# First attention of an attention and feed-forward kernel: maximum and sums through TensorE products

## The chip, the core and the metric

The kernel runs on one core of one Trainium2 chip. The metric is the device time of one execution, in microseconds (us). A profiled execution also has a span, from its first to its last instruction in the trace; all starts in the rows below count from the span's start.

## What is computed

For every batch b (8), and every head (8 heads, 64 wide, 576 tokens), the reference makes 32 "memories" and attends over them; then all tokens go through a feed-forward layer.

```python
a = phi - max(phi over tokens); a = exp(a); a = a / (sum over tokens + 1e-9)
k_m = a.T @ k;  v_m = a.T @ v                    # 32 x 64 per head
scores = (q @ k_m.T) / 8                         # 576 x 32 per head
scores = scores - max(scores over the 32)
attn = exp(scores); attn = attn / (sum over the 32 + 1e-9)
x = heads side by side of (attn @ v_m)           # 4608 x 512
out = max(x @ w_in, 0) ** 2 @ w_out              # w_in 512 x 2048, w_out 2048 x 512
```

## The kernel before, in words

Tokens are worked in 16 half-batches (b, t) of T = 288. The partitions of an attention tile hold 4 heads x 32 memories: "half" 0 and 1 are the even and odd heads of the four pairs, so one half-batch's attention is a tile of 128 x (2 x 288). `attn @ v_m @ w_in` is regrouped: `u = v_m @ w_in` is made per batch (`make_u`, L514), and `ffn1` (L642) multiplies it by the attention; `ffn2` (L669) multiplies the squared result by w_out. Weights arrive packed and are decoded on chip (`decode`, L545): ScalarE writes two intermediate tiles (L556, L559), VectorE reworks one (L563, L565, L568), and VectorE or GpSimd adds them (L575).

The time around the change is the start, before the first `ffn1`. It is written out by hand as generators, advanced in the order of one string (L1265): `e` is the softmax over tokens of batch 0, `m` its memories, `d0`, `d1`, `d2` three decodings of w_in, `o0` one of w_out, `a0` and `a1` the attention of half-batches (0, 0) and (0, 1), `u0` and `v0` two parts of u for batch 0, and `s` a spin.

```python
"e e e e e m m d0 m m d0 a0 a0 d1 a0 s d1 d0 a0 d1 s d2 a0 u0 d2 a0 u0 d2 s a1 o0 o0 v0 v0 s"
```

Each engine issues its instructions in the order in which this string brings them to it, and waits in order. A spin (`spin`, L148) is a product of the identity with itself that nothing reads. An fp32 product is two TensorE instructions (load and product each), so `spin(1)` is two instructions of 512 columns, and the eight products of `by_heads` (L418) are sixteen.

The first attention before, `attend` (L430), in six steps for `a0`: scores by `by_heads` into two PSUM banks (TensorE); two block transposes out of PSUM (L443) and the maximum over blocks of 32 (L448), then four spins; the subtraction (L453, VectorE here); the exponential (L455, ScalarE); the sum, eps, reciprocal (L458 to L460), two spins, the multiplication (L463); and the transposition back (L468). The result is the fp32 tile `a_hi2`, which `ffn1` reads. While the start lasts, `new_ps` (L131) hands out PSUM banks `acc0`/`acc1` and `acc2`/`acc3` in turns.

The start ends in three products that the first feed-forward steps need: the attention tile (L468), the second part of u (`v0`, L424 and L525, behind the addition of `d2`, L575), and the first decoded w_out (`o0`, whose addition L575 comes right after the string).

Of the kernel before, what the change touches and what calls it, by code (L numbers as in the profile page):

```python
# [9 lines left out]
F32 = mybir.dt.float32  # L10
# [3 lines left out]
AF = mybir.ActivationFunctionType  # L14
ALU = mybir.AluOpType
AX = mybir.AxisListType
# [9 lines left out]
def attn_moe_kernel(ctx: ExitStack, tc: tile.TileContext, qT, kv, phi, w_in, w_out, outT):  # L26
# [12 lines left out]
    nc = tc.nc  # L39
    ctx.enter_context(tc.manual_schedule())  # L40

    B, NQ, S = kv.shape[:3]
    P = 128
    DM = outT.shape[0]
    NPAIR = 2 * NQ
    DFF = w_out.shape[0]
    D = 64
    M = 32
    NFT = DFF // P
    NET = DM // P  # L50
    T = S // 2
# [9 lines left out]
    EPS = 1e-9  # L61
    SCALE = 1.0 / float(D) ** 0.5
# [4 lines left out]
    const = ctx.enter_context(tc.tile_pool(name="const", bufs=1))  # L67
    work = ctx.enter_context(tc.tile_pool(name="work", bufs=2))
    one = ctx.enter_context(tc.tile_pool(name="one", bufs=1))
    dram = ctx.enter_context(tc.tile_pool(name="dram", bufs=1, space=bass.MemoryType.DRAM))  # L70
    ps_acc = ctx.enter_context(tc.tile_pool(name="ps_acc", bufs=1, space=PSUM))
    ps_h = ctx.enter_context(tc.tile_pool(name="ps_h", bufs=2, space=PSUM))
# [3 lines left out]
    ident = const.tile([P, P], F32, name="ident")  # L76
# [45 lines left out]

    eps = const.tile([P, NQ * NBLK], F32, name="eps")
    nc.gpsimd.memset(eps, EPS)

    kv_used = set()
    starting = [True]
# [3 lines left out]
    def new_ps(main=False):  # L131

        if starting and not main:
            n = len(starting) - 1
            starting.append(True)
            return [ps_acc.tile([P, 512], F32, name=f"acc{2 * (n % 2) + i}") for i in range(2)]
        assert not ps_user, (now, ps_user)
        ps_user.append(list(now))
        return ps_m.tile([P, 2, 512], F32, name="ps_m")

    def done_ps(ps):
        if not isinstance(ps, list):
            ps_user.pop()

    def bank(ps, i):
        return ps[i] if isinstance(ps, list) else ps[:, i]

    def spin(n, x):  # L148

        h = ps_h.tile([P, 512], F32, name="h")  # L150
        for _ in range(n):
            nc.tensor.matmul(h, x, ident[:, None, :].broadcast_to([P, 4, P]), start=True, stop=True)
# [38 lines left out]
    def exp_phi(b, e):  # L191

        w = NQ * P
        mx = chunk_max(e)
        yield
        ps = new_ps()
        tp, bc = bank(ps, 0), bank(ps, 1)
        for qd in range(NQ):
            nc.tensor.transpose(tp[:, qd * P:(qd + 1) * P], mx[:, qd * P:(qd + 1) * P], ident)
        yield  # L200
        nmx = work.tile([P, NQ], F32, name="nmx")
        nc.vector.tensor_reduce(
            out=nmx, in_=tp[:, :w].rearrange("p (q x) -> p q x", q=NQ), axis=AX.X, op=ALU.max, negate=True
        )
        yield
        for qd in range(NQ):
            nc.tensor.matmul(
                bc[:, qd * P:(qd + 1) * P], nmx[:, qd:qd + 1].broadcast_to([P, P]), ident,
                start=True, stop=True,
            )  # L210
        if starting:
            spin(1, nmx[:, :1].broadcast_to([P, P]))
        yield
        if starting:
            for x in e:
                n = x.shape[0]
                nc.vector.tensor_tensor(out=x, in0=x, in1=bc[:n, :w], op=ALU.add)
                nc.scalar.activation(x, x, AF.Exp)
        else:
            n = e[4].shape[0]  # L220
            nc.vector.tensor_tensor(
                out=e_sb[:, :4], in0=e_sb[:, :4], in1=bc[:, None, :w].broadcast_to([P, 4, w]), op=ALU.add
            )
            nc.vector.tensor_tensor(out=e[4], in0=e[4], in1=bc[:n, :w], op=ALU.add)
        done_ps(ps)
        if starting:
            ready.add(("phi", b))
            return
        yield
        nfull = S // P  # L230
        nc.scalar.activation(e_sb[:, :nfull], e_sb[:, :nfull], AF.Exp)
        if nfull < NCH:
            nc.scalar.activation(e[nfull], e[nfull], AF.Exp)
        ready.add(("phi", b))
# [60 lines left out]
    def memories(b, e, kvs, mem):  # L295
# [6 lines left out]
        sums = [(ps_h.tile([P, 512], F32, name="h") if qd else tp) if not b else accs[qd][:, 2 * D:] for qd in range(NQ)]  # L302
# [39 lines left out]
        if two:  # L342
            n = rows(NCH - 1)
            for j in range(4):
                for qd in range(NQ):
                    y = kvs[qd][-1] if qd else kvs[qd][-1][:n]
# [22 lines left out]
        for qd in turns:  # L369
            x = accs[qd][:, :2 * D].rearrange("p (x d) -> p x d", x=2)[:, :, None, :].broadcast_to([P, 2, 2, D])  # L370
# [9 lines left out]
        if b > 2:  # L380
            done_ps(ps)
            for j in range(4):
                if j == 2 or j and b > JOIN:
                    yield
                for k in range(2):
                    for x in range(2):
                        at = M * (2 * (j % 2) + k)
# [12 lines left out]
        for half, copy in ((0, nc.scalar.copy if b == 1 else nc.vector.tensor_copy), (1, nc.scalar.copy)):  # L400
            hs = slice(D * half, D * (half + 1))
            copy(mem[hs], tp[hs].rearrange("p (x r h m) -> p x r h m", x=2, r=NPAIR, h=2)[:, :, :, half])
        done_ps(ps)
        ready.add(("mem", b))

    def load_q(b, t):
        if (b, t) in ((0, 1), (1, 1)):
            x = [const.tile([P, NQ, T], F32, name=n) for n in ("a_hi3", "a_lo3")]
        else:
            x = one.tile([P, NPAIR, T], F32, name="q_sb")  # L410
            x = [x[:, :NQ], x[:, NQ:]]
        for i in range(2):
            nc.sync.dma_start(
                out=x[i], in_=qT[b, NQ * i:NQ * (i + 1), :, t * T:(t + 1) * T].rearrange("a p s -> p a s")
            )
        return x

    def by_heads(out, mem, x, rhs):  # L418

        for pr in range(NPAIR):  # L420
            for half in range(2):
                hs = slice(D * half, D * (half + 1))
                y = rhs[pr // NQ][hs, pr % NQ]
                nc.tensor.matmul(  # L424
                    bank(out, half)[M * pr:M * (pr + 1), :y.shape[-1]], mem[hs, x, pr], y, start=True, stop=True
                )
# [65 lines left out]
    def new_a():  # L492
        i = a_slots.take()
        return (const.tile([P, NQ, T], F32R, name=f"a_hi{i}"), const.tile([P, NQ, T], F32R, name=f"a_lo{i}"), i)
# [8 lines left out]
    ready = set()  # L503
# [92 lines left out]
    def decode_in(n, q0, q1, adder=nc.gpsimd):  # L596

        def new_out():
            if n // 2 not in w_in_at:
                w_in_at[n // 2] = new_w()  # L600
            return w_in_at[n // 2][:, 2 * q0:2 * q1, n % 2 * HC:n % 2 * HC + HC]

        assert all(("in", n, qd) in fetched for qd in range(q0, q1))
        yield from decode(raws["in", n][:, q0:q1], new_out, adder, ("in", n, q0))
        ready.update(("in", n, qd) for qd in range(q0, q1))
        if all(("in", n ^ i, x) in ready for i in range(2) for x in range(NQ)):
            if starting:
                kept.append(n // 2)
                return
            yield  # L610
            keep_w(n // 2)

    def decode_out(k, adder=nc.gpsimd, whole=False):

        def new_out():
            w = room(k, [P, 2, DM], F32)
            wo[2 * k:2 * k + 2] = [w[:, 0], w[:, 1]]
            return w

        assert all(("out", k, i) in fetched for i in range(2))  # L620
        w = yield from decode(raws.pop(("out", k)), new_out if whole else None, adder, ("out", k))
        if not whole:
            yield
            yield from split(k, w.rearrange("p (i x) -> p i x", i=2))
        ready.update(("out", 2 * k + i) for i in range(2))
# [475 lines left out]
    state = {b: {"a32": {}, "q": {}, "u": {}, "a": [None] * NT, "kv": {}} for b in range(B)}  # L1101
# [16 lines left out]
    def task_mem(b, kvs=None):  # L1118
        kvs = kvs or [state[b]["kv"][qd] for qd in range(NQ)]
        new_mem(b)  # L1120
        return memories(b, [e_sb[:, c] for c in range(NCH)], kvs, state[b]["mem"])
# [6 lines left out]
    def task_attend(b, t):  # L1128
        def new():
            state[b]["a"][t] = new_a()  # L1130
            return state[b]["a"][t]

        return attend(b, t, state[b]["q"].pop(t), state[b]["mem"], new)
# [14 lines left out]
    def task_u(b, n, n0=0, n1=FC):  # L1148
        got = state[b]["u"].setdefault(n, [])
        w = w_at.pop((b, n)) if (b, n) in w_at else w_in_at[n]  # L1150
        if (b, n) not in streamed:
            assert all(("in", 2 * n + i, qd) in ready for i in range(n0 // HC, n1 // HC) for qd in range(NQ))
        return make_u(b, n, state[b]["mem"], (n0, n1, w), got)

    full = {0}
    unsplit = {(0, 0): "a_hi2", (0, 1): "u_lo0"}
# [28 lines left out]
    st = state[0]  # L1185
# [59 lines left out]
    for fn, *args in loads[:later]:  # L1245
# [5 lines left out]
    start = {  # L1251
        "e": lambda: exp_phi(0, st["phi"]),
        "m": lambda: task_mem(0, kvs),
        "d0": lambda: decode_in(0, 0, 1),
        "d1": lambda: decode_in(0, 1, 2),
        "d2": lambda: decode_in(1, 0, 2, nc.vector),
        "o0": lambda: decode_out(0, nc.vector, True),
        "v0": lambda: task_u(0, 0, HC, 2 * HC),
        "a0": lambda: task_attend(0, 0),
        "a1": lambda: task_attend(0, 1),  # L1260
        "u0": lambda: task_u(0, 0, 0, HC),
    }
# [175 lines left out]
    for k, step in enumerate(steps):  # L1438
        i, b, t, f = step
# [57 lines left out]
    for j in range(-1, LAST + 1):  # L1497
# [29 lines left out]
        if new:  # L1527
            ffn1_product(u1, j + 1, 1, True)
            ffn1_product(z, j + 1, 2, True)
            x = from_z(j + 1, 2, *(("g_hi", 3) if old else ("r", 2)))  # L1530
# [99 lines left out]
```

## Time and profile before

| | |
|---|---|
| time, median of 3 runs | 703.32 us (702.68 to 704.96) |
| time of the profiled execution | 703.33 us |
| its span | 701.5 us |
| TensorE products busy | 688.9 us (98%) |
| TensorE weight loads busy | 568.9 us (81%) |
| VectorE busy | 517.6 us (74%) |
| ScalarE busy | 407.2 us (58%) |
| GpSimd busy | 353.3 us (50%) |

TensorE's weight loads run beside its products. A busy TensorE is not one at its peak, since products are pipelined and the time of one (272 ns) is longer than the distance to the next. An engine's share over the whole span says little of one stage; the rows below are mostly of the first 50 us. "Idle before" in brackets names what the trace takes for the releaser of a wait.

### The profile page before, as it was taken

To read this page: it belongs to the slowest core of one execution; us is meant where nothing else is said; L and a number is where in the kernel's file an instruction comes from. 1 tells how busy PE (TensorE), PEld (TensorE's weight loads), DVE (VectorE), ACT (ScalarE), POOL (GpSimd) and SP (SyncE) were. 2 spreads that over 40 slices of the span, in tenths; PEclk is the share of its full clock that TensorE was granted. 3 is DMA by queue.
4 is the path that set the end of the run, shared out by engine and by line. 5 is a ranking of instruction groups with operands and counts; after the bars stand their busy time and mean duration, and the time that the engine had idled before them with its cause. 6 is when DMAs were issued, how large, how long until landed. Compare 5 with 4: busy or idle time off the path is not lost.

```text
span 701.5 us, 13957 instructions
## 1 busy us (share of the span) xinstructions
PE 688.9 (98%) x5030; PEld 568.9 (81%) x5030; DVE 517.6 (74%) x1138; ACT 407.2 (58%) x1117; POOL 353.3 (50%) x527
## 2 busy tenths in 40 slices
PE   7889999999999999999999999999999999999997
PEld 3367889899998887888788878877888778888897
DVE  3977759644775979988798979887998876765432
ACT  2566888876455455655565456655565556554531
POOL 1122345443376557745774568555764577555100
PEclk9999999999999999999999999999999999999999
DMA  9996154704346561069114911375105300400101
GB/s 300 356 348 242 58 191 129 249 1 139 119 100 208 149 179 60 16 198 231 44 56 154 257 71 61 112 215 155 62 26 189 91 28 37 146 36 0 47 15 45
DMA packets 65365, 89.83 MB, mean 128 GB/s; under 512 B 6928, under 2 KB 53584, under 8 KB 61712
## 3 DMA queue, kind: packets, MB, share of 16 engines
q1 hardware_dynamic: 63408, 87.41, 39.6%
q10 hardware_dynamic: 1888, 1.54, 0.7%
q8 instruction: 39, 0.64, 0.4%
q14 instruction: 30, 0.25, 0.1%
HBM read 75.30 MB, written 13.63 MB: 127 GB/s over the span
## 4 chain that ended last, share of the span: by engine, by line
PE 92%; DMA 4%; DVE 2%; ACT 0%; issue 0%; SPq 0%; DVEq 0%; ACTq 0%
PE acc L1004 39%; PE h L1028 11%; PE acc L682 10%; PE z L1028 8%; PE h L653 7%; PE acc L674 4%; PE m L424 4%; PE h L1580 2%; DMA wp<-in_w_in 1%; PE ps_m L424 1%; DMA wp<-in_w_out 1%; PE m L1580 1%; PE z L1580 1%; DMA kvb<-in_kv 1%; PE m L316 1%; PE acc L1469 1%
## 5 line engine op out<-in xcount | busy, mean ns | idle before, releaser
L1004 PE MATMUL acc<-u_hi,wp 128*128 128x512 f32 x576 | 154.4, 399 | 0.0
L1004 PE MATMUL acc<-u_lo,wp 128*128 128x512 f32 x576 | 147.7, 392 | 0.0
L1004 PEld LDWEIGHTS acc<-u_hi,wp 128*128 128x128 f32 x576 | 103.8, 188 | 41.4 <-issue 24.1
L1004 PEld LDWEIGHTS acc<-u_lo,wp 128*128 128x128 f32 x576 | 105.6, 188 | 18.4
L909 POOL TENSOR_TENSOR u_lo<-low,u_hi 128x256 fp32r<-128x256 f32 (+1 forms) x134 | 84.8, 644 | 51.7 <-ACT u_hi L908 50.4
L1052 POOL TENSOR_TENSOR u_hi<-g_lo,u_hi 128x288 fp32r<-128x288 f32 (+1 forms) x82 | 64.7, 789 | 73.5 <-ACT g_lo L1049 50.8
L666 POOL TENSOR_TENSOR g_lo<-g,g_hi 128x288 fp32r<-128x288 f32 x48 | 44.5, 929 | 65.6 <-ACT g_hi L664 51.4
L908 ACT CAST u_hi<-low 128x256 fp32r<-128x256 f32 (+1 forms) x160 | 51.9, 347 | 43.7 <-POOL low L920 21.0
L682 PE MATMUL acc<-g_hi,wp 128*128 128x288 f32 x360 | 58.7, 297 | 0.9 <-DVE o L1085 0.9
L1047 ACT ACTIVATE u_hi<-g_hi 128x224 fp32r<-128x224 f32 x95 | 39.0, 410 | 35.0 <-DVE g_hi L1044 35.0
L682 PEld LDWEIGHTS acc<-g_hi,wp 128*128 128x128 f32 x360 | 51.1, 188 | 5.3 <-issue 2.6
L1044 DVE CUSTOM_DVE_ANT_0 g_hi<-h,g_hi 128x288 f32<-128x288 f32 x95 | 42.7, 450 | 4.9 <-ACT g_hi L1075 4.2
L655 ACT ACTIVATE r<-h 128x288 f32<-128x288 f32 x64 | 26.1, 407 | 33.7 <-PE h L653 33.4
L1052 POOL TENSOR_TENSOR u_lo<-g_lo,u_lo 128x224 fp32r<-128x224 f32 x30 | 21.5, 715 | 38.3 <-ACT g_lo L1049 36.5
L1075 ACT COPY g_hi<-z 128x288 f32<-128x288 f32 x48 | 19.1, 397 | 28.7 <-PE z L1028 28.6
L1028 PE MATMUL z<-a_hi,u_hi 128*128 128x288 f32 x120 | 35.3, 294 | 0.0
L1028 PE MATMUL h<-a_lo,u_hi 128*128 128x288 f32 x120 | 34.6, 295 | 0.0
L682 PE MATMUL acc<-g_lo,wp 128*128 128x288 f32 x180 | 34.6, 295 | 0.0
L674 PE MATMUL acc<-g_hi,wp 128*128 128x288 f32 x128 | 34.0, 410 | 0.6 <-DVE wp L575 0.6
L1067 ACT ACTIVATE u_lo<-g 128x288 fp32r<-128x288 f32 x48 | 21.4, 446 | 22.3 <-DVE g L1063 22.1
L1028 PE MATMUL h<-w_sb,u_hi 128*128 128x288 f32 x120 | 34.1, 296 | 0.0
L1069 DVE TENSOR_TENSOR g_lo<-h,g 128x288 f32<-128x288 f32 x48 | 21.8, 454 | 14.9 <-ACT g L1065 13.3
(340 smaller groups left out, 1785.4 us busy)
## 6 DMA issues: line engine op xcount, KB each, us to landing
w_sb<-w_f SPq DMA_DIRECT2D x24, 1024.0 KB, 5.0
wp<-in_w_in SPq DMA_DIRECT2D x16, 512.0 KB, 7.8
wp<-in_w_out SPq DMA_DIRECT2D x16, 512.0 KB, 7.1
q_sb<-in_q SPq DMA_DIRECT2D x28, 288.0 KB, 5.6
kvb<-in_kv SPq DMA_DIRECT2D x28, 256.0 KB, 6.3
tmp<-in_kv SPq DMA_DIRECT2D x24, 256.0 KB, 5.9
w_f<-w_sb SPq DMA_DIRECT2D x4, 1024.0 KB, 5.0
e_sb<-in_phi SPq DMA_DIRECT2D x7, 512.0 KB, 6.5
```

The costliest lines, as they stand in the source:

```text
L424: nc.tensor.matmul(bank(out, half)[M * pr:M * (pr + 1), :y.shape[-1]], mem[hs, x, pr], y, start=True, stop=True)
L653: nc.tensor.matmul(h[:, :T], u[:, qd, fs], x[:, qd], start=(i == 0), stop=(i == len(todo) - 1))
L666: nc.gpsimd.tensor_tensor(out=g_lo, in0=g, in1=g_hi.bitcast(F32), op=ALU.subtract)
L674: nc.tensor.matmul(acc[e][:, :T], wo[f][:, e * P:(e + 1) * P], g_hi, start=first, stop=last)
L682: nc.tensor.matmul(acc[e][:, :T], wo[f][:, w, e * P:(e + 1) * P], x, start=first and x is g_hi and w == 0, stop=last and x is g_lo,)
L908: nc.scalar.copy(hi[:, k], x)
L909: by(name, p).tensor_tensor(out=lo[:, k], in0=x, in1=hi[:, k].bitcast(F32), op=ALU.subtract)
L1004: nc.tensor.matmul(late_accs[e], wo[f][:, w, e * P:(e + 1) * P], x, start=f == 0 and first, stop=f == NFT - 1 and last,)
L1028: nc.tensor.matmul(out[:, :T], u[:, lhs], a, start=first and not n, stop=n == 2, skip_group_check=not first)
L1044: nc.vector._custom_dve(TENSOR_ADD_SAT, out=x, in0=u[:, :T], in1=x, s0=float("inf"), s1=0.0)
L1047: nc.scalar.square(g_hi, x[:, :n])
L1052: by(f"c{k}", p).tensor_tensor(out=g_lo, in0=g[:, :n], in1=g_hi.bitcast(F32), op=ALU.subtract)
```

## The change

`a0` calls a new generator `first_attend` in place of `attend`; nothing else moves in the order string. It has five steps where `attend` had six, and the sixth `a0` of the string does nothing.

1. TensorE: 24 products with 96 tokens as stationary columns (64 partitions) and 32 memories as moving columns, so that scores stand with tokens on partitions (`by_token`); then the old scores (`by_heads`) into the other two banks; then a spin.
2. VectorE: two maxima over blocks of 32 straight from PSUM, 96 x 384 each, negated. TensorE: `spread`, 24 products (32 stationary columns, 96 moving) that add the negated maximum onto the old scores in PSUM; then a spin.
3. ScalarE: two exponentials from PSUM, 128 x 288 each. TensorE: 6 products with 96 stationary columns and 4 moving ones (`heads`, a 0/1 matrix) that give the sums with tokens on partitions.
4. VectorE: add eps, reciprocal, on 96 x 24. TensorE: `spread` again, 24 products, into two banks.
5. VectorE: two multiplications, PSUM by SBUF, 128 x 288 each, into `a_hi2`.

Five memsets on GpSimd at the start make `heads`.

```diff
+    heads = const.tile([P, P // M], F32, name="heads")
+    nc.gpsimd.memset(heads, 0.0)
+    for g in range(P // M):
+        nc.gpsimd.memset(heads[M * g:M * (g + 1), g:g + 1], 1.0)
...
+    def first_attend(q, mem):
...
+        C = 3
+        R = T // C
+        G = P // M
+        by_token = new_ps()
+        for c in range(C):
+            for pr in range(NPAIR):
+                for half in range(2):
+                    hs = slice(D * half, D * (half + 1))
+                    at = M * (G * c + pr)
+                    nc.tensor.matmul(
+                        bank(by_token, half)[:R, at:at + M], q[pr // NQ][hs, pr % NQ, R * c:R * (c + 1)], mem[hs, 0, pr],
+                        start=True, stop=True,
+                    )
+        sc = new_ps()
+        by_heads(sc, mem, 0, q)
+        spin(1, ident)
+        yield
+        mx = const.tile([P, 2, C, G], F32, name="tops")
+        for half in range(2):
+            y = bank(by_token, half)[:R, :C * P].rearrange("t (c g m) -> t c g m", c=C, g=G)
+            nc.vector.tensor_reduce(out=mx[:R, half], in_=y, axis=AX.X, op=ALU.max, negate=True)
+
+        def spread(out, x, **kw):
+            for half in range(2):
+                for c in range(C):
+                    for g in range(G):
+                        nc.tensor.matmul(
+                            bank(out, half)[M * g:M * (g + 1), R * c:R * (c + 1)],
+                            x[:R, half, c, g:g + 1].broadcast_to([R, M]), ident[:R, :R], stop=True, **kw
+                        )
+
+        spread(sc, mx, start=False, skip_group_check=True)
+        spin(1, ident)
+        yield
+        y = one.tile([P, 2, T], F32, name="st")
+        for half in range(2):
+            nc.scalar.activation(y[:, half], bank(sc, half)[:, :T], AF.Exp, scale=SCALE)
+        sums = ps_h.tile([P, 512], F32, name="h")[:R, :2 * C * G].rearrange("t (h c g) -> t h c g", h=2, c=C)
+        for half in range(2):
+            for c in range(C):
+                nc.tensor.matmul(sums[:, half, c], y[:, half, R * c:R * (c + 1)], heads, start=True, stop=True)
+        yield
+        nc.vector.tensor_scalar_add(mx[:R], sums, EPS)
+        nc.vector.reciprocal(mx[:R], mx[:R])
+        out = new_ps()
+        spread(out, mx, start=True)
+        yield
+        at = const.tile([P, NQ, T], F32, name=unsplit[0, 0])
+        state[0]["a32"][0] = at
+        for half in range(2):
+            nc.vector.tensor_tensor(out=at[:, half], in0=bank(out, half)[:, :T], in1=y[:, half], op=ALU.mult)
+        ready.add(("a32", 0, 0))
...
-        "a0": lambda: task_attend(0, 0),
+        "a0": lambda: first_attend(state[0]["q"].pop(0), state[0]["mem"]),
```

## Rows read from the trace of the kernel before

**Rows 1.** The page's part 2, forty equal slices of the span

```profile
PE   7889999999999999999999999999999999999997
...
DVE  3977759644775979988798979887998876765432
```

**Rows 2.** Stretches: length, busy us of PE, PEld, DVE, ACT, POOL; PEclk

```profile
18.50:22.00 3.50, 3.37 (x9) 1.25 (x8) 3.36 (x8) 1.76 (x3) 1.27 (x1) 1.00 1.04 402
...
41.00:46.50 5.50, 3.79 (x126) 2.96 (x124) 5.35 (x7) 2.95 (x6) 0.00 (x0) 1.00 1.04 378
46.50:60.00 13.50, 13.50 (x88) 9.00 (x96) 8.97 (x15) 8.87 (x19) 4.90 (x3) 1.00 0.93 350
```

**Rows 3.** The chain that ended last: start us, us, what

```profile
32.03 1.23 DVE wp L575
...
41.04 1.22 DVE e_sb L221
...
46.49 2.21 PE acc L674 x8
```

**Rows 4.** Timeline (start us, us), VectorE: first attention and a decoding

```profile
18.43 0.84 DVE L443 STREAM_TRANSPOSE st<-acc 128x288 f32<-128x288 f32 x2
...
23.86 0.27 DVE L460 RECIPROCAL sm<-sm 128x18 f32<-128x18 f32 x1
...
24.16 0.76 DVE L463 TENSOR_TENSOR st<-st,sm 128x576 f32<-128x576 f32 x1
...
24.83 0.69 DVE L563 TENSOR_SCALAR tmp<-tmp 128x1024 f32<-128x1024 f32 x1
...
27.43 0.77 DVE L468 STREAM_TRANSPOSE a_hi<-st 128x576 f32<-128x576 f32 x1
...
28.12 1.18 DVE L575 CUSTOM_DVE_ANT_0 w_sb<-tmp,low 128x2048 uint16<-128x2048 uint16 x1
```

**Rows 5.** Timeline, TensorE's weight loads: scores, and a spin between scores

```profile
17.44 0.18 PEld L424 LDWEIGHTS acc<-q_sb,mem 64*32 64x32 f32 x14 [0.27 <-ACT mem L402]
...
18.09 0.30 PEld L152 LDWEIGHTS h<-ident 128*128 128x128 f32 x2 [0.46 <-issue]
...
26.75 0.30 PEld L152 LDWEIGHTS h<-ident 128*128 128x128 f32 x2 [0.41 <-issue]
...
27.80 0.12 PEld L424 LDWEIGHTS acc<-a_hi,mem 64*32 64x32 f32 x4 [0.76 <-DMA e_sb<-in_phi]
```

**Rows 6.** Timeline, TensorE: products with 32 stationary columns

```profile
13.72 0.28 PE L307 MATMUL h<-ones,e_sb 128*32 128x2 f32 x16
...
13.85 0.41 PE L316 MATMUL acc<-u_lo,e_sb 128*32 128x128 f32 x8
...
14.29 0.28 PE L307 MATMUL h<-ones,e_sb 128*32 128x2 f32 x16
```

**Rows 7.** Timeline, TensorE: four loads of 128 columns

```profile
7.22 0.52 PEld L207 LDWEIGHTS acc<-ident,nmx 128*128 128x128 f32 x4 [0.75 <-DVE nmx L202]
```

**Rows 8.** One tile's instructions, ns min/median/max: narrow loads and products

```profile
L316 PEld LDWEIGHTS acc<-wp,e_sb x40: 106/110/110, 10.3 to 14.7; 128*32 128x32 f32 x40
L316 PE MATMUL acc<-wp,e_sb x40: 272/273/297, 10.3 to 14.8; 128*32 128x128 f32 x40
```

**Rows 9.** Timeline and page: prices of single instructions

```profile
6.74 0.42 DVE L202 TENSOR_REDUCE nmx<-acc 128x2 f32<-128x256 f32 x1 [0.58 <-PE acc L199]
...
32.18 0.41 ACT L655 ACTIVATE r<-h 128x288 f32<-128x288 f32 x1 [1.13 <-PE h L653]
...
L1069 DVE TENSOR_TENSOR g_lo<-h,g 128x288 f32<-128x288 f32 x48 | 21.8, 454 | 14.9 <-ACT g L1065 13.3
```

**Rows 10.** Timeline: GpSimd at the start, ScalarE at the second decoding

```profile
1.28 0.12 POOL L124 MEMSET eps<- 128x18 f32 x1
...
18.69 1.27 POOL L575 TENSOR_TENSOR w_sb<-tmp,low 128x512 int32<-128x512 int32 x1 [15.15 <-DVE tmp L568]
...
22.41 1.15 ACT L556 ACTIVATE tmp<-wp 128x1024 f32<-128x1024 f32 x1 [0.85 <-DMA wp<-in_w_in]
```

More of the change, by code (lines that the diff above doesn't have):

```diff
@@ L404, in memories @@
         ready.add(("mem", b))
+    def first_attend(q, mem):
+        assert ("mem", 0) in ready
+        C = 3
[48 more added lines that the diff above has]
+        ready.add(("a32", 0, 0))
```

## The prediction, made before the changed kernel ran

> **What bounds the kernel now.** I read the forty slices first [rows 1]: TensorE is at 9 from the fourth slice to the last but one, so only the first 50 us have room, and there VectorE is the busy one (a 9 in the second slice). The stretches of the start say it sharper [rows 2]: from 41.0 to 46.5 us VectorE works 5.35 of 5.5 us and TensorE 3.79; from 46.5 us TensorE is busy without a gap. The chain that ended last [rows 3] then shows VectorE's addition for w_out at 32.03, its work for batch 1 at 41.04, and TensorE from 46.49 on. So whatever moves VectorE's line before 33 us moves the end by the same amount: behind it stand VectorE's own queue and then a full TensorE. (Earlier pieces of the chain name DMA transfers. I don't take these as waits: VectorE's instructions follow one another there without idle time.)
>
> The place to watch is the second large decoding, `d2`. Its first VectorE instruction begins at 24.83, right behind the first attention's multiplication at 24.16; its addition begins at 28.12, behind the transposition L468 [rows 4]. `v0` and `o0` follow that addition in order. I measure the change by when that addition can begin.
>
> **What is removed.** Nine VectorE instructions of `a0` (L443 twice, the last L468, 0.77 us) [rows 4], 5.6 us of VectorE together, and four of the six spins inside `a0`. In the old kernel no step of `a0` made VectorE wait: its transposes began at 18.43, when VectorE came free of `d0`.
>
> **What is added.** VectorE gets two maxima, an addition, a reciprocal and two multiplications. The maxima: 256 columns from PSUM took 0.42 us; for 384 I take 0.55 each (bounds 0.42, and 0.63 by straight scaling). The multiplications have a twin in L1069, 288 columns with one PSUM operand, 0.45 us each [rows 9]. The reciprocal cost 0.27 [rows 4]; the addition has no more columns, 0.2. In sum 2.5 us, so VectorE's work falls by 3.1 us. But each new step sits behind TensorE, VectorE keeps its order, and everything behind a waiting instruction waits too: `d1` behind the maxima, `d2` behind the multiplications. So the new line is TensorE's, and I add it up.
>
> *Start.* The products need the second half of `mem`, copied by ScalarE; the scores' loads went on at 17.44 [rows 5]. The same holds now.
>
> *By token.* 48 instructions, each with a load of 96 columns on 64 partitions. No row has this shape. Four loads of 128 columns span 0.52 us with 0.19 for the last, 111 ns apart [rows 7], or 0.87 ns a column: 83 ns for 96 columns. The moving side, 32 columns, is shorter than that. Loads into separate tiles of the array do overlap: sixteen products of 32 stationary columns passed in 0.13 us, 8 ns apart, though one load lasts 110 ns [rows 6, 8]; and 14 loads on two halves of the rows spanned 0.18 us [rows 5]. Even and odd heads lie on the two halves and alternate, so I take two at a time: 48 x 83 / 2 = 2.0 us, ending at 19.5. Bounds: 48 x 8 ns = 0.4 us, and 48 x 111 ns = 5.3 us. I take the value between because the load is nearest in width to [rows 7] and in placing to [rows 5]. [...]
>
> *Scores, spin.* The old scores again: 0.65 us from 17.44 to the next load at 18.09. A spin: 26.75 to 27.80, 1.05 us [rows 5]. That is 21.2 us. Beside it run the maxima: a product's result comes 0.16 us after its streaming (273 ns [rows 8] against four times 27 ns [rows 6]), so 19.7 + 1.1 = 20.8: hidden by the spin. `d1`, behind them on VectorE, takes about half of `d2`'s 2.5 us (24.83 to 28.12 without L468) and is done near 22.1, GpSimd's addition for it 1.3 us later [rows 4, 10]: early enough for all that follows.
>
> *First spread.* 48 instructions of 96 columns over four column tiles. Sixteen with 128 columns plus their change-over fill 13.85 to 14.29, 27 ns each [rows 6]; scaled to 96 columns 21 ns: 1.0 us, and 0.1 to change over; ends at 22.3. (Bounds 8 and 29 ns.) *Spin*: 23.35. The exponentials, 0.41 us each [rows 9], start half by half and end at 22.9: hidden by this spin. ScalarE then goes to `d2`, whose data landed only at 22.41 [rows 10]; a start at 22.9 ends its first pass at 24.1, before VectorE asks.
>
> *Sums.* 12 instructions with 96-column loads on all rows, nothing to overlap with: 12 x 83 ns = 1.0 us, 24.35 (bounds 0.1 and 1.3). The addition and reciprocal follow until about 25.0, hidden by the `s` spin, which ends at 25.4. *Second spread*: 1.1 us, 26.5; result and hand-over 0.2; the last multiplication 0.45 (the first runs beside the spread's second half): 27.2.
>
> So `d2` begins on VectorE at 27.2 where it began at 24.83: 2.35 us later. Between it and its addition L468 is gone, 0.77 us: the addition is **1.6 us later**. ScalarE's second pass for it has ended by then (its buffer comes free when GpSimd ends `d1`, near 23.4). On TensorE, `u0`'s products stand behind the second spread and one spin; they too are later, but `v0` behind them waits for the addition of `d2` in any case. Nothing behind gives this back: VectorE's queue from `o0` to 46.5 us is the same work in the same order [rows 2, 3].
>
> *At nothing:* the five memsets, 0.1 us each like the one at 1.28, on a GpSimd that later idles for 15.15 us before 18.69 [rows 10]; uncovered they would cost 0.6 us. No DMA is added or moved on any queue, and the first scores of `a1`, which take the next pair of banks, come after the exponentials.
>
> **Sum.** 703.3 + 1.6 = **704.9 us**, against the profiled execution's 703.33 (span 701.5 and 1.8 around it), which is also the median of the runs. About 0.3%, 2.1 us, is what a measurement of this kernel can tell from no change: I forecast a loss below that. By the pitches' spread, half a microsecond in by-token and about as much in the rest, this case's own range is 703.9 to 705.9.
>
> **Rivals.** *Slower: the wide loads don't overlap.* The place is the by-token products. If a 96-column load holds the array's load path alone, 48 x 83 ns = 4.0 us, 2.0 more; the maxima no longer hide, and all behind moves: 3.6 us later, 706.9 us. It decides from 52 ns an instruction (by token 2.5 us, a loss of 2.1). For it: the path for wide loads isn't shown shared in any row. Against: narrow loads overlap in both directions. [...]
>
> *Faster or equal: the products are as cheap as the narrow ones.* By token 0.4 us and sums 0.4 us; then VectorE's maxima set the pace (18.43 + 1.1 = 19.5), and by the same sum `d2` begins at 25.0 and its addition 0.6 us earlier: 702.7 us. At the far end VectorE's saving would count until ScalarE's first pass of `d2`, 22.41 + 1.15 = 23.56 [rows 10]: 1.3 + 0.77 = 2.0 us, 701.3. For it: the 8 ns of narrow products [rows 6]. Against: a load four times as long is not in those rows.
>
> *The clock falls.* [...] The new stretch has fewer spins, small products and waits. [...] Against: by my sum TensorE waits nowhere for long.
>
> **Chances.** Forecast 0.57, serial loads 0.21, cheap products 0.17 (0.05 of it near its far end), clock 0.05. Slower by over 0.3% (above 705.4): the serial case, the clock, and a sixth of the forecast: 0.36. Faster by over 0.3% (below 701.2): only the far end, 0.05. Within: 0.59. The range that leaves out 2 in 10 goes from the cheap case to just beyond the serial one: 702.4 to 707.2.
>
> **What would show it.** Right: by-token products some 42 ns apart, ending near 19.5; VectorE idle for about a microsecond before the maxima, and again, some 2 us in all, before the sums' addition and the multiplications, with TensorE as the releaser; L563 of `d2` near 27.2 and its addition near 29.7; the first `ffn2` 1.6 us after its old place, and the same distance at 46.5 us. Wrong: by-token spacing of 8 or of 80 ns; maxima that end after the spin; a granted clock below 1.00 between 17 and 30 us; or a shift at 30 us that is no longer there at 60 us, which would mean that VectorE's line was not what the end hung on.

## The result, and the profile after

The changed kernel took 710.86 us (median of 4 runs, 710.36 to 710.96); the kernel before took 703.87 (median of the three runs of the table above and one more). The ratio is 1.0098 with an interval of 1.0079 to 1.0117: 5.6 to 8.2 us slower. I had said 704.9 and at most 707.2. In a run in which TensorE's granted clock fell the time is longer (one kernel below took 704.12 to 704.46 us at 1.000, and in the median 707.96 at 0.995 to 0.998); since that is one of the causes here, runs are told apart by the clock that each lists.

The page of the changed kernel, part 2, against [rows 1]: the same picture, but the second slice has a PEclk of 8, and VectorE has fallen from 9 to 5 there.

```profile
PE   7989999999999999999999999999999999999997
...
DVE  3597659744866878988798879887997877755432
...
PEclk9899999999999999999999999999999999999999
```

The stretches behind it (length, then busy us and number of instructions of PE, PEld, DVE, ACT, POOL, then the granted clock, DMA share and GB/s), to set beside [rows 2]:

```profile
17.00:18.50 1.50, 1.50 (x32) 1.50 (x32) 0.73 (x2) 0.15 (x1) 0.56 (x1) 0.81 1.09 384
18.50:22.00 3.50, 3.50 (x34) 1.76 (x32) 2.24 (x5) 1.18 (x2) 0.71 (x1) 0.50 1.04 403
22.00:26.00 4.00, 4.00 (x55) 2.48 (x54) 0.23 (x1) 1.45 (x3) 1.78 (x2) 0.65 1.03 391
26.00:31.00 5.00, 5.00 (x80) 2.78 (x80) 2.75 (x7) 1.67 (x3) 0.00 (x0) 1.00 1.08 341
```

The reader is to see three things in them. The granted clock is 0.50 for all of 18.5 to 22.0, and partly before and after (0.81 and 0.65). TensorE is busy for every microsecond of it (3.50 of 3.50), so no wait of TensorE shows. VectorE works 0.23 of the 4 us from 22 to 26: it waits, and it is TensorE that it waits for (4.70 us before the addition, L456 below). A cut at 17.95 and at 24.78 gives a clock of 0.50 throughout those 6.83 us.

The timeline of the same stretch (start us, us, engine, line; L423 by-token loads, L434 maxima, L157 spins, L440 spread, L454 sums, L456 addition, L464 multiplications, L624 the first VectorE instruction of `d2`, L636 its addition, L735 the first product of the second layer):

```profile
16.69 2.84 PEld L423 LDWEIGHTS acc<-mem,q_sb 64*96 64x96 f32 x46 [0.16 <-ACT mem L407]
...
19.69 1.02 DVE L434 TENSOR_REDUCE tops<-acc 96x12 f32<-96x384 f32 x2 [1.93 <-PE acc L423]
...
20.74 2.07 PE L157 MATMUL h<-ident 128*128 128x512 f32 x2
...
22.74 2.15 PE L440 MATMUL acc<-ident,tops 96*32 96x96 f32 x48
...
24.82 1.13 PE L157 MATMUL h<-ident 128*128 128x512 f32 x2
...
25.79 1.10 PE L454 MATMUL h<-heads,st 128*96 128x4 f32 x12
...
26.93 0.18 DVE L456 TENSOR_SCALAR tops<-h 96x24 f32<-96x24 f32 x1 [4.70 <-PE h L454]
...
27.78 1.20 PE L440 MATMUL acc<-ident,tops 96*32 96x96 f32 x48
28.62 0.95 DVE L464 TENSOR_TENSOR a_hi<-acc,st 128x288 f32<-128x288 f32 x2 [1.18 <-PE acc L440]
...
29.49 0.68 DVE L624 TENSOR_SCALAR tmp<-tmp 128x1024 f32<-128x1024 f32 x1
...
32.33 1.23 DVE L636 CUSTOM_DVE_ANT_0 w_sb<-tmp,low 128x2048 uint16<-128x2048 uint16 x1 [0.17 <-PE acc L485]
...
37.66 2.18 PE L735 MATMUL acc<-g_hi,wp 128*128 128x288 f32 x8 [0.29 <-DVE wp L636]
```

The first spin lasts 2.07 us and the first spread 2.15; the second ones, after 24.8, 1.13 and 1.20. `d2` begins at 29.49, where it began at 24.83 [rows 4]; the first second-layer product comes at 37.66, where it came at 33.41: 4.25 us later. The line of that product in the kernel before:

```profile
33.41 2.18 PE L674 MATMUL acc<-g_hi,wp 128*128 128x288 f32 x8 [0.29 <-DVE wp L575]
```

That distance lies unchanged in the chain where VectorE's line ends and TensorE's begins, 50.75 against 46.49 [rows 3]:

```profile
49.47 1.24 DVE wp L636
...
50.75 2.21 PE acc L735 x8
```

But the span is 708.5 us against 701.5: 7.0 us. Another 2.75 us are lost later, and not in a wait. They are in the 1152 products of 512 columns, which took 399 and 392 ns each before (the two groups, `u_hi` and `u_lo`) and now take 401 and 394, 1.3 us of busy time more in each group. Before, then after:

```profile
L1004 PE MATMUL acc<-u_hi,wp 128*128 128x512 f32 x576 | 154.4, 399 | 0.0
L1004 PE MATMUL acc<-u_lo,wp 128*128 128x512 f32 x576 | 147.7, 392 | 0.0
```

```profile
L1065 PE MATMUL acc<-u_hi,wp 128*128 128x512 f32 x576 | 155.7, 401 | 0.0
L1065 PE MATMUL acc<-u_lo,wp 128*128 128x512 f32 x576 | 149.0, 394 | 0.0
```

So there were three losses to explain, and only one of them was in my sum.

### The profile page after: what moved, and what is told of

It is laid out like the page before. It is cut to its first block, busy times and chain, and to the rows that moved or that the text cites. A ratio compares the mean times of both kernels' runs of the same rounds, so it can differ in the third digit from the quotient of the medians.

```text
span 708.5 us, 14256 instructions
## 1 busy us (share of the span) xinstructions
PE 695.9 (98%) x5178; PEld 575.5 (81%) x5178; DVE 514.1 (73%) x1135; ACT 407.1 (57%) x1118; POOL 353.8 (50%) x532
## 4 chain that ended last, share of the span: by engine, by line
PE 95%; DVE 3%; DMA 1%; ACT 0%; issue 0%; SPq 0%; DVEq 0%; ACTq 0%
PE acc L1065 39%; PE h L1089 11%; PE acc L743 10%; PE z L1089 8%; PE h L714 7%; PE acc L735 4%; PE m L485 4%; PE h L1641 2%; PE ps_m L485 1%; PE z L1641 1%; PE m L1641 1%; PE h L157 1%; PE m L321 1%; PE acc L1530 1%; PE h L321 1%; PE h L485 1%
## 5 line engine op out<-in xcount | busy, mean ns | idle before, releaser
L735 PE MATMUL acc<-g_hi,wp 128*128 128x288 f32 x128 | 34.0, 410 | 0.6 <-DVE wp L636 0.6
L1108 ACT ACTIVATE u_lo<-g 128x224 fp32r<-128x224 f32 x48 | 18.7, 390 | 24.5 <-DVE g L1105 24.5
```

The costliest lines, as they stand in the source:

```text
L735: nc.tensor.matmul(acc[e][:, :T], wo[f][:, e * P:(e + 1) * P], g_hi, start=first, stop=last)
L1108: nc.scalar.square(g_hi, x[:, :n])
```

## The experiments

**The kernel before, again, beside the next three.**

> The kernel before, taken again beside the next three, for a trace of the same chip. The changed kernel's trace is 4.25 us late at the first product of the second feed-forward layer (37.66 against 33.41) and 7.0 us late at the end of the span. Either theory below explains the 4.25. If the other 2.75 us belong to the change, this trace ends at 701.5 us again and its TensorE pieces between 100 and 600 us are as long as in the first trace of before. If they are a difference between chips, the span here is some 2 to 3 us longer than 701.5 with the start up to 50 us the same, that is 703.5 to 704.5.

It took 704.44 us, span 702.6; seven other runs on this chip have a median of 702.61 with a clock of 0.999 or 1.000, and this one 0.997. Its 512-column products last as long as in the first trace, and its shift against that trace stays between 1.03 and 1.17 us from 75 us to the end. So the steady loss belongs to the change. The trace also shows the old kernel losing its clock (0.55 from 18.5 to 22.0), in an execution in which q came late, 1.41 us of waiting for its DMA (timeline, then a stretch):

```profile
17.72 1.54 PE L424 MATMUL acc<-q_sb,mem 64*32 64x288 f32 x16 [1.41 <-DMA q_sb<-in_q]
...
19.20 3.49 PE L152 MATMUL h<-ident 128*128 128x512 f32 x4
```

```profile
18.50:22.00 3.50, 3.50 (x12) 1.34 (x13) 2.63 (x5) 1.47 (x3) 1.24 (x1) 0.55 1.06 403
```

**A spin ahead of the by-token products** (clock or chain?).

```diff
+        spin(2, ident)
         by_token = new_ps()
```

> The changed kernel with two spins (four instructions of 512 columns) ahead of the by-token products; nothing else. Theory A, the clock: in the changed kernel the granted clock fell to 0.50 at 17.95 us and stayed there for 6.83 us, and this cost half of it, 3.4 us, because TensorE's line was what all waited for. The spins keep the clock at 1.00; they run from 15.8 to 17.7 where TensorE waited until 16.69 for the memories, so they delay by 1.1 us and win 3.4: some 2.3 us faster than the changed kernel, 708.6. By-token products 85 ns a pair to their end. Theory B, the chain: the clock's fall slows work that had room, and the loss is the line of steps by itself: then the spins only delay, 1.1 us slower, 712.

Measured 708.54 us (4 runs, all with a clock of 1.000): 2.3 us less than the changed kernel, with two spins more. That is theory A's number; B's was 712. The changed kernel was not run again beside it, but the two traces say the same: `d2` begins at 27.35 in place of 29.49, 2.14 us earlier. All 48 by-token loads now pass in 2.12 us, the spread in 1.20:

```profile
17.70 2.12 PEld L424 LDWEIGHTS acc<-mem,q_sb 64*96 64x96 f32 x48 [0.76 <-DVE tmp L627]
...
20.50 1.12 PE L157 MATMUL h<-ident 128*128 128x512 f32 x2
...
21.56 1.20 PE L441 MATMUL acc<-ident,tops 96*32 96x96 f32 x48
...
27.35 0.68 DVE L625 TENSOR_SCALAR tmp<-tmp 128x1024 f32<-128x1024 f32 x1
```

```profile
17.00:18.50 1.50, 1.50 (x22) 0.80 (x20) 0.99 (x2) 0.68 (x1) 0.29 (x1) 1.00 1.10 373
18.50:22.00 3.50, 3.50 (x73) 2.24 (x75) 1.97 (x5) 0.67 (x1) 0.97 (x1) 1.00 1.04 411
```

**The first spin moved there.**

```diff
+        spin(1, ident)
         by_token = new_ps()
...
         by_heads(sc, mem, 0, q)
-        spin(1, ident)
```

> The changed kernel with the first spin moved from behind the scores to ahead of the by-token products. Theory A (clock): the clock holds, 3.4 us won, the spin's 0.95 us are off the line behind the scores, 0.2 us lost ahead: some 4.1 us faster than the changed kernel, 706.7; and if what is left is my sum of the chain, that is 1 to 2 us above the kernel before on the same chip. If one spin is too little, the clock still falls, later. Theory B: 0.7 us faster, 710.1.

Measured 706.21 us: 4.65 us less than the changed kernel, where A said 4.1 and B 0.7. One spin is enough here (the clock was 1.000 in all four runs):

```profile
16.44:18.70 2.26, 2.26 (x49) 2.22 (x48) 1.12 (x3) 0.72 (x2) 0.90 (x1) 1.00 1.07 373
18.70:25.60 6.90, 6.90 (x131) 4.14 (x130) 4.23 (x10) 3.68 (x5) 2.17 (x3) 1.00 1.03 401
```

And this trace has the second-layer product at 33.31 us, before the 33.41 of the kernel before, and still ends 2.9 us later (span 704.4). The start alone could no longer explain the loss.

```profile
27.99 1.23 DVE L636 CUSTOM_DVE_ANT_0 w_sb<-tmp,low 128x2048 uint16<-128x2048 uint16 x1 [0.17 <-PE acc L485]
...
33.31 2.18 PE L735 MATMUL acc<-g_hi,wp 128*128 128x288 f32 x8 [0.29 <-DVE wp L636]
```

**Even heads before odd heads** (do wide loads overlap?), on top of the moved spin.

```diff
-        for c in range(C):
-            for pr in range(NPAIR):
-                for half in range(2):
+        for half in range(2):
+            for c in range(C):
+                for pr in range(NPAIR):
```

> As the kernel with the spin moved, and the by-token products of all even heads before those of the odd heads, so that neighbours lie on the same half of the rows. In the changed kernel pairs are 85 ns apart at the full clock, two products in each. If the two halves of the array load side by side, neighbours are now 85 ns apart singly, the 48 take 4.1 us in place of 2.0, and the time is 2.0 us above the kernel with the spin moved (the clock may fall too, since TensorE streams less; then up to 3.4 us more). If loads wait only for a common path, 43 ns each as before and the same time.

711.24 us, 5.0 more than with the spin moved. The doubled length makes about 2.0 of it by the expectation; the rest, about 3, goes with the clock, which fell in all four runs (0.990 to 0.997). This division is worked out and not measured, and that the clock fell because TensorE streamed less was my guess, which no run shows. Its 48 loads span 4.52 us, against 2.23 with the halves in turn:

```profile
16.36 4.52 PEld L424 LDWEIGHTS acc<-mem,q_sb 64*96 64x96 f32 x48 [0.76 <-DVE tmp L624]
```

By the single starts of these loads, while the clock was full (1.00 until 18.5 us), the overlap that I assumed for 96 columns is real: two products every 85 ns if they lie on different halves of the rows, one if not.

**The kernel before with the two new tiles and nothing else** (the steady loss).

```diff
+    heads = const.tile([P, P // M], F32, name="heads")
...
+            tops = const.tile([P, 2, 3, 4], F32, name="tops")
+            nc.gpsimd.memset(tops, 0.0)
```

> The kernel before with its own first attention, and only the two new constant tiles (16 and 96 bytes a partition) allocated at the same places as in the change and written by memsets on GpSimd. With the spin moved the first product of the second layer began at 33.31 us (before 33.41), and still the span was 2.9 us longer: the loss grows steadily from 60 us on, 2 ns in each of the 1152 products of 512 columns. Theory P, placement: the new tiles move the weights' tiles wp2 to wp5 and wp0 by 32 bytes a partition and all later tiles by 128, and TensorE reads its operands a little slower there. Then this kernel is 2.8 us slower than the kernel before. Theory Q: the steady loss comes with the new attention itself (other instructions, other code length): then it is within 0.3 us of before.

705.87 us against 702.52: ratio 1.0042 (1.0027 to 1.0056), 3.0 us by the ratio (3.4 between the medians). Theory P. The old attention, with 112 bytes a partition allocated, written and never read, has the same slow products as the changed kernel:

```profile
L1012 PE MATMUL acc<-u_hi,wp 128*128 128x512 f32 x576 | 155.6, 401 | 0.0
L1012 PE MATMUL acc<-u_lo,wp 128*128 128x512 f32 x576 | 149.0, 394 | 0.0
```

**The change without new room: spin moved, and the change as it is.**

```diff
-    heads = const.tile([P, P // M], F32, name="heads")
+    eps_heads = const.tile([P, NQ * NBLK + P // M], F32, name="eps")
+    eps, heads = eps_heads[:, :NQ * NBLK], eps_heads[:, NQ * NBLK:]
...
-        mx = const.tile([P, 2, C, G], F32, name="tops")
+        mx = one.tile([P, 2 * C * G], F32, name="mx").rearrange("p (h c g) -> p h c g", h=2, c=C)
```

> The changed kernel with the spin moved, and with the 0/1 matrix in the unused bytes behind eps and the maxima in the room of the old tile mx, so that all weights' tiles and all operands of the 512-column products lie where they lay before. P: 2.8 us faster than the kernel with the spin moved, so 0.8 us above before (my sum of 1.6 less the 0.95 of the spin, with 0.15 for its new place): 703.4. Q: as the kernel with the spin moved, 3.6 us above before.

> The changed kernel as it is, only with the two tiles packed into rooms that were there. P and the clock: 2.8 us less than the changed kernel; what is left over before is the chain 1.6 and the clock 3.4, 5.0 us: 707.6. Q: no change, 8 us over before.

With the spin moved: 703.95 us, ratio 1.0018 (1.0001 to 1.0035), expected 703.4; the products are back at 399 and 392:

```profile
L1064 PE MATMUL acc<-u_hi,wp 128*128 128x512 f32 x576 | 154.4, 399 | 0.0
L1064 PE MATMUL acc<-u_lo,wp 128*128 128x512 f32 x576 | 147.7, 392 | 0.0
```

The change as it is: 707.20 us, ratio 1.0051 (1.0033 to 1.0069), expected 707.6. This kernel separates the other two losses by itself, since its clock did not fall in every run. Three of 12 runs list 1.000 and took 704.12 to 704.46; nine list 0.995 to 0.998, with a median of 707.96. The old kernel beside it: 29 of 35 runs at 0.999 or 1.000, median 702.47; six below, median 704.94. So the chain alone, at the full clock, costs 704.42 - 702.47 = 1.95 us by these three runs (my sum: 1.6), and the clock's fall 3.5 us in this kernel. The loss goes with the lost clock: the five runs at 0.995 have a median of 708.19, 3.8 us above the three, and the four at 0.997 and 0.998 one of 706.3, 1.9 us above. Its trace is of a run with the fall:

```profile
17.00:18.50 1.50, 1.50 (x24) 1.50 (x25) 0.91 (x2) 0.52 (x1) 0.38 (x1) 0.56 1.06 369
18.50:22.00 3.50, 3.50 (x43) 2.52 (x42) 1.57 (x4) 0.82 (x2) 0.89 (x1) 0.50 1.05 401
22.00:26.00 4.00, 4.00 (x54) 1.84 (x54) 0.91 (x2) 1.29 (x3) 1.78 (x2) 0.75 1.03 398
```

**Decoding ahead of the multiplications** (can the gain be had?), with spin moved and tiles packed.

```diff
-        "... d0 a0 d1 s d2 a0 u0 d2 a0 u0 d2 s a1 ..."
+        "... d0 a0 d1 s d2 d2 u0 d2 a0 u0 s a1 ..."
```

> As the kernel with spin moved and tiles packed, with the second decoding ahead of the multiplications on VectorE: in the order string d2 d2 u0 d2 a0 u0 in place of d2 a0 u0 d2 a0 u0 d2. In the trace with the spin moved VectorE stood idle from 23.0 to 24.3 us for the second spread; d2's input is ready on ScalarE near 23.6. If my reading holds that VectorE waits in order for a step that d2 doesn't need, d2's addition begins 1.7 us earlier and the multiplications end where VectorE's work alone puts them: some 1.8 us faster than the kernel with the packed tiles, about 1 us faster than the kernel before, 701.7. If TensorE's line sets the start anyway, no gain.

702.57 us, ratio 1.0001 (0.9984 to 1.0019): 1.4 us less than with `d2` behind (1.8 expected), and no better than before (about 1 us expected). `d2` did begin on VectorE at 23.52, but its addition (L635) waited 0.70 us:

```profile
23.52 0.78 DVE L623 TENSOR_SCALAR tmp<-tmp 128x1024 f32<-128x1024 f32 x1
...
26.99 1.22 DVE L635 CUSTOM_DVE_ANT_0 w_sb<-tmp,low 128x2048 uint16<-128x2048 uint16 x1 [0.70 <-PE ps_m L484]
...
33.05 2.18 PE L734 MATMUL acc<-g_hi,wp 128*128 128x288 f32 x8 [1.02 <-ACT g_hi L719]
```

**The same with u0's products in place of a spin.**

```diff
-        "... d0 a0 d1 s d2 d2 u0 d2 a0 u0 s a1 ..."
+        "... d0 d1 a0 u0 d2 d2 d2 a0 u0 s a1 ..."
```

> As the kernel with the decoding ahead, and u0's products on TensorE in place of the second of its two order-string spins, ahead of the second spread. In the trace of the kernel with the decoding ahead, d2's addition waited 0.7 us for u0's products, which read the same tile. If that wait was on the line, 0.7 us faster than that kernel, 701.9, with the clock at 1.00; if the missing spins let the clock fall, up to 3.9 us slower, and more often.

In the trace u0's products now stand right behind the second spread, at 24.43 in place of 26.13 us, and not ahead of it as the expectation says; one spin is gone.

702.12 us, ratio 0.9985 (0.9970 to 1.0001), beside a kernel before of 703.01. The wait is down from 0.70 to 0.17 us, so u0's reading of the same tile had held the addition. It begins 0.9 us earlier; 0.53 of that is the wait, the rest an earlier start of `d2`. Whether this version beats the kernel before isn't settled: the interval just takes in no change. Its clock fell in one run of 12.

```profile
24.43 0.66 PE L484 MATMUL ps_m<-w_sb,mem 64*32 64x256 f32 x16
...
26.11 1.23 DVE L635 CUSTOM_DVE_ANT_0 w_sb<-tmp,low 128x2048 uint16<-128x2048 uint16 x1 [0.17 <-DVE tmp L628]
...
32.16 2.18 PE L734 MATMUL acc<-g_hi,wp 128*128 128x288 f32 x8 [1.02 <-ACT g_hi L719]
```

**Which placement counts?** One tile of 32 bytes, unused, in the kernel before: ahead of all weights, or behind `wp0`.

```diff
+    pad = const.tile([P, 8], F32, name="pad")
+    nc.gpsimd.memset(pad, 0.0)
```

> The kernel before with one unused constant tile of 32 bytes ahead of the weights: the weights' tiles and the moving tiles of the 512-column products all move by 32 bytes a partition, that is from 32 to 0 modulo 64. In the padded kernel the products whose next weights lie in the tiles moved by 32 took 3.5 ns more (233.6 against 230.1), those whose weights and moving tile both moved by 128 took 0.3 ns more. Theory W: weights at 0 modulo 64 are slower wherever the moving tile lies: then all 1152 products lose 3.5 ns, 4.0 us slower than before. Theory D: what counts is that weights and moving tile lie differently modulo 64: then no loss.

> The kernel before with the same tile after wp0: wp2 to wp5 and wp0 stay at 32 modulo 64, the moving tiles and wp1, wp6, wp7 go to 0. Theory W: the 432 products with wp1, wp6, wp7 lose 3.5 ns, 1.5 us slower than before. Theory D: the 720 products with the five tiles that stay lose, 2.5 us slower, the other 432 don't.

All by 32: 702.88 us, ratio 0.9999 (0.9988 to 1.0010), which is theory D; W had 4.0 us. The later ones alone: 705.23 us, ratio 1.0030 (1.0019 to 1.0041), 2.1 us. That time, 1.3 to 2.9 us by its interval, takes in both W's 1.5 and D's 2.5; there the grouping by tile below decides for D. The product groups of the first, then of the second:

```profile
L1006 PE MATMUL acc<-u_hi,wp 128*128 128x512 f32 x576 | 154.3, 399 | 0.0
L1006 PE MATMUL acc<-u_lo,wp 128*128 128x512 f32 x576 | 147.7, 392 | 0.0
```

```profile
L1007 PE MATMUL acc<-u_hi,wp 128*128 128x512 f32 x576 | 155.6, 401 | 0.0
L1007 PE MATMUL acc<-u_lo,wp 128*128 128x512 f32 x576 | 148.7, 393 | 0.0
```

The grouping by tile is worked out from the starts of these products, whose order in the code tells which weights are loaded during each (mean ns from start to start, 587 and 370 products, those that the next one followed within 300 ns):

```
                         next weights in wp0, wp2 to wp5    in wp1, wp6, wp7
before                   230.0                              229.6
change                   233.6                              230.0
before, padded           233.7                              230.0
change, packed           230.0                              229.6
all moved by 32          229.9                              229.6
only the later by 32     232.9                              230.1
```

Before, the weights' tiles and the moving tiles all lie at 32 modulo 64 bytes. In the change the first five weights' tiles moved by 32 bytes (the 16 of `heads`, rounded up); the other three, and the moving tiles, moved by 128 or another multiple of 64. The five then lie at 0 modulo 64 and the moving tiles at 32. With 32 and 0 the loss is nearly the same; with 0 and 0 there is none. That the period is 64 is not shown: no run has them 64 bytes apart. Nor is it shown that the next weights count and not those in use: for all but 23 of the 957 products both lie in the same group of tiles, and those 23 don't decide it.

## Why the prediction was wrong

**The sum of the chain was right.** At the full clock and with the old placement the change costs 1.95 us by three runs, where the sum gave 1.6. From the first by-token load to `d2`'s first instruction the trace with the spin added, where the clock stayed at 1.00, has 9.65 us (17.70 to 27.35), and the sum had 9.76 (17.44 to 27.2). Its terms in the same trace: by-token loads 2.12 us (2.0 forecast), spread 1.20 with its result (1.1 and 0.16), a spin 1.12 (1.05); the maxima took 1.02 (1.1). That VectorE loses by waiting in order what it saves in work, and that the loss passes whole from `d2` to TensorE's last line, held: the shift of 4.25 at the first second-layer product is 4.26 us at 50.75.

**The step that failed first: "TensorE waits nowhere for long", as the argument against the falling clock.** I gave that case 0.05. That waiting is what makes the clock fall was my assumption, and no run shows it. TensorE indeed did not wait: in the stretch from 17.02 to 17.95, right before the fall, it was busy 0.93 of 0.93 us. But what it was busy with were weight loads, with 32 columns streamed for each, behind a stretch of small products and two waits for the memories (0.75 and 0.16 us). The loads 17 to 18 us, then from 18 us on, of the changed kernel:

```profile
16.86 1.10 PEld L423 LDWEIGHTS acc<-mem,q_sb 64*96 64x96 f32 x22
...
17.95 1.58 PEld L423 LDWEIGHTS acc<-mem,q_sb 64*96 64x96 f32 x18
```

22 loads in 1.10 us and 18 in 1.58. By their single starts, pairs are 85 ns apart until 17.87 and 160 ns from 17.95 on: the forecast's 42 ns each at a granted clock of 0.99 to 1.00, and the same work at 0.50. (The 80 ns a product that were to be a sign of serial loads did come, but from the clock.) Scores, spin (2.07 us against 1.13 for the second one) and spread (2.15 against 1.20) at about half pace complete the 6.83 us; of these I take half as lost, 3.4 us, an estimate from the clock of 0.50. Between the runs of one kernel it was 3.5. The chance that I gave it was too small. In the order of the work the two kernels differ here: behind its scores the old one ran four dense spins, and the new one begins with 48 loads and has one spin after them.

**The step that failed second: "At nothing: the five memsets".** I priced the instructions and not the room of the tiles that they write. No rival held this: the new tiles moved the weights relative to the moving operands, which cost 2.7 us between the runs at a clock of 0.994 to 0.995 of the change (710.86) and of the change packed (708.19, run later), and 3.0 us in the padded kernel before.

Taken each from its own comparison, 1.95 for the chain, 3.4 for the clock (half of 6.83) and 3.0 for the placement make 8.35 us. From 702.5, the old kernel with its clock up, to 710.86 it is 8.4. That they meet so closely is partly luck: by the comparison that one takes, the clock is 3.4 to 3.8 and the placement 2.7 to 3.4. In the first pair of traces the start shows less than chain and clock, 4.25 in place of 5.0 to 5.35; 0.75 of this is that the memories were ready earlier in the second: the by-token loads went on at 16.69 where the scores' loads went on at 17.44 [rows 5].

**The rivals.** Serial loads: excluded, since two loads passed in 85 ns with the halves in turn and one with the halves apart (48 in 2.23 and in 4.52 us). Cheap products: excluded by the same pitch (a load of 96 columns is three times as wide as those of 32 in [rows 6], not four). VectorE's waits before the maxima, the sums' addition and the multiplications were 1.93, 4.70 and 1.18 us, and at the full clock (spin moved, tiles packed) 1.08, 1.34 and 1.18, where I had written one and two more. That u0's products do no harm behind the second spread held for the change as it is, where `d2`'s addition waited 0.17 us; with `d2` early it no longer did, and its addition waited 0.70 us for them.

What stays open: what exactly in TensorE's work before 17.95 let the clock fall. A spin ahead of the by-token products kept it in all 8 runs of two kernels; with the same spin it still fell in 3 of 12 with the tiles packed, and in all 4 with the halves apart. Which load of work is enough was not tried.

## What to carry to other kernels

Work that moves from a loaded engine to a waiting one has to be priced as a line of hand-overs in order, and what stands behind each wait moves with it; a reordering that lets other work fill the wait was worth 1.4 us here, as much as the new chain had cost with its spin moved. If dense products are taken out of a stretch and loads or narrow products put in, read the granted clock there first: a busy TensorE is not a sign that it keeps its clock (0.50 here, busy 3.50 of 3.50 us). And a new constant tile can move everything allocated behind it (3.0 us in the padded kernel): put it into unused bytes, as was done here, or look whether the groups of unchanged products still have their old mean.

## What the runs showed of the hardware that was not expected

The pace of 512-column products depended on how the weights lie against the columns that are streamed (those in use or those loaded for the next product, the runs don't tell): 229.6 to 230.1 ns from start to start in the runs in which both lie at 32 or both at 0 modulo 64 bytes, 232.9 to 233.7 in those in which one lies at 32 and the other at 0, whichever of the two is at 0. With 720 of the 1152 products so placed, two kernels that change nothing else (later by 32; padded) lost 2.1 and 3.0 us in 703. Other distances were not tried.

The clock fell to 0.50 while TensorE was busy without a gap (6.83 of 6.83 us), and by these runs it is partly a matter of chance: the same program (the change packed) lists 1.000 in three runs and 0.995 to 0.998 in nine. The kernel before has it too, in 6 of 35 and in 5 of 29 runs (median 704.9 and 704.7 against 702.5 and 702.7), so part of the spread of its times is this.
